# One ring of eight PSUM banks, the last batch's mixing among the first product's matmuls, and u's differences made in the front

## The chip, the cores and the metric

The kernel runs on one core of a Trainium2 chip. The metric is the device time of one execution in microseconds (us); the profiled span of an execution is 1.8 to 2.1 us shorter than its time.

## The reference, cut to what matters

Causal linear attention with decay (4 batches, 8 heads, 768 positions, head size 64), then a mixer: a low-rank product over the positions, and two large products with a ReLU between them.

```python
x = attention(q, k, v, lam)            # (4, 768, 512), heads side by side
h = x.transpose(0, 2, 1) @ U @ V       # rank 32, mixes the positions of one batch
u = x + h.transpose(0, 2, 1)
out = u + np.maximum(u @ w_ch1, 0.0) @ w_ch2     # 512 -> 2048 -> 512
```

## The kernel before

The kernel has a front (attention and mixing, in 24 steps of 128 positions), a first product (u with w_ch1) and a second. Both products are kept accurate by splitting an operand into a high part and a rest: two matmuls per block into pz, and a third into pd with the small difference u_d. Batches 0 and 1 run interleaved with a lag of one batch, and so do 2 and 3, so that one batch's attention lies beside the other's mixing.

The mixing of a batch and the turn of one step into the first product's operand:

```python
def tmp(name):                       # shared by pt, pt_h, ut, uf, wt, wl and others
    return wconv.tile([P, C], FP32, tag="tmp", bufs=3, name=name)
...
pts[b] = tmp("pt")                   # low(b): x times U for a batch, evicted by ScalarE
nc.scalar.copy(pts[b], pp)
...
nc.tensor.matmul(out=pr, lhsT=gather..., rhs=pts.pop(b), ...)      # low_sum(b)
t = tmp("pt_h")
nc.vector.tensor_scalar(t..., pr..., HI, None, ALU.bitwise_and)
nc.scalar.copy(p_hl[0 : P // 2], t[0 : P // 2])
nc.vector.tensor_tensor(out=p_hl[P // 2 : P], in0=pr[P // 2 : P], in1=t[P // 2 : P], op=ALU.subtract)
...
nc.tensor.matmul(out=pu, lhsT=v_hl[:, ...], rhs=p_hl, ...)         # mix(s)
nc.vector.tensor_tensor(out=xs[s], in0=pu, in1=xs[s], op=ALU.add)
...
pt = mbank([P, CT, P], "put")        # turn(s): four transposes of x_nat
t = tmp("ut")...
nc.vector.tensor_scalar(t..., pt..., HI, None, ALU.bitwise_and)
nc.scalar.copy(uhl[g][:, 0, :, cols], t)
nc.vector.tensor_tensor(out=uhl[g][:, 1, :, cols], in0=pt, in1=t, op=ALU.subtract)
```

PSUM in the front is three rings: two banks for scores, three for attention, three for the rest. The differences are made by VectorE when the first product begins, ahead of each pair's first unit:

```python
def u_diff(g):
    for ct in range(CT):
        nc.vector.scalar_tensor_tensor(ud[g][:, ct, :], hi[:, ct, :], E, low[:, ct, :],
                                       ALU.mult, ALU.subtract)
```

## Time and profile before

| | before |
|---|---|
| median of 4 runs (lowest to highest) | 737.38 us (735.95 to 738.01) |
| profiled span, granted clock | 736.8 us, 0.981 |
| first pu (batch 0's mixing begins) | 78.64 us |
| last transposes of u (put) of batch 1's mixing | 119.46 us |
| pr of the last batch (its mixing alone is left) | 174.23 us |
| first matmul pz of the first product | 187.71 us |

All boundaries are starts of instructions on TensorE's timeline. The time from the first pu to the last put of batch 1, 40.8 us here, is called the stretch below: two batches are mixed in it, beside the attention of one or two others.

### The profile page before, as it was taken

To read this page: it belongs to the slowest core of one execution; us is meant where nothing else is said; L and a number is where in the kernel's file an instruction comes from. 1 tells how busy PE (TensorE), PEld (TensorE's weight loads), DVE (VectorE), ACT (ScalarE), POOL (GpSimd) and SP (SyncE) were. 2 spreads that over 40 slices of the span, in tenths; PEclk is the share of its full clock that TensorE was granted. 3 is DMA by queue.
4 is the path that set the end of the run, shared out by engine and by line. 5 is a ranking of instruction groups with operands and counts; after the bars stand their busy time and mean duration, and the time that the engine had idled before them with its cause. 6 is when DMAs were issued, how large, how long until landed. Compare 5 with 4: busy or idle time off the path is not lost.

```text
span 736.8 us, 11337 instructions
## 1 busy us (share of the span) xinstructions
PE 706.1 (96%) x4176; PEld 567.9 (77%) x4176; DVE 514.3 (70%) x903; ACT 300.2 (41%) x525; POOL 87.6 (12%) x74
## 2 busy tenths in 40 slices
PE   5789999997899999999999999999999999999997
PEld 4677778874688888888888888888888888888885
DVE  4544997467999867777777924578668686676864
ACT  2554656655346555455445612223232232322320
POOL 2323214330300000000000000003002030110300
PEclk9979999998899999999999999999999999999999
DMA  9876767722247665556556689985536344363431
GB/s 155 172 158 156 188 163 183 156 76 103 97 143 269 232 213 186 210 190 223 194 211 228 229 314 309 346 314 167 162 90 211 96 159 146 101 187 100 159 98 57
DMA packets 131807, 131.76 MB, mean 179 GB/s; under 512 B 81320, under 2 KB 89512, under 8 KB 131752
## 3 DMA queue, kind: packets, MB, share of 16 engines
q1 hardware_dynamic: 131752, 131.04, 57.4%
q8 instruction: 33, 0.54, 0.3%
q14 instruction: 22, 0.18, 0.1%
HBM read 80.68 MB, written 50.33 MB: 178 GB/s over the span
## 4 chain that ended last, share of the span: by engine, by line
PE 87%; DVE 5%; ACT 3%; DMA 2%; issue 1%; POOL 1%; SPq 1%; DVEq 0%; ACTq 0%; POOLq 0%
PE pz L541 24%; PE pd L547 12%; PE pz L643 12%; PE pz L642 12%; PE pd L644 12%; PE ps L293 3%; PE px L315 3%; PE px L310 2%; DMA words<-in_moe_V_dram 1%; PE pk L261 1%; PE pkv L331 1%; DVE sm L298 1%; PE pq L261 1%; PE pxn L355 1%; PE put L405 1%
## 5 line engine op out<-in xcount | busy, mean ns | idle before, releaser
L541 PE MATMUL pz<-u_hl,w 128*128 128x512 f32 x768 | 187.8, 397 | 0.0
L541 PEld LDWEIGHTS pz<-u_hl,w 128*128 128x128 f32 x768 | 144.7, 189 | 35.2
L643 PE MATMUL pz<-w_hl,m 128*128 128x512 f32 x384 | 152.2, 396 | 0.0
L644 PE MATMUL pd<-w_d,m 128*128 128x512 f32 x384 | 152.2, 396 | 0.0
L642 PE MATMUL pz<-w_hl,m 128*128 128x512 f32 x384 | 152.2, 396 | 0.0
L627 ACT ACTIVATE m<-mt 128x512 fp32r<-128x512 f32 x96 | 60.6, 632 | 192.5 <-PE pd L644 132.3
L628 DVE SCALAR_TENSOR_TENSOR m<-rm,m 128x512 fp32r<-128x512 f32 x96 | 71.4, 746 | 50.6 <-ACT m L627 50.3
L555 DVE SCALAR_TENSOR_TENSOR r<-pd,r 128x512 f32<-128x512 f32 x96 | 61.7, 685 | 62.4 <-ACT r L554 54.1
L547 PE MATMUL pd<-u_d,w 128*128 128x512 f32 x384 | 99.4, 401 | 2.9 <-DVE u_d L530 2.9
L554 ACT ACTIVATE r<-pz 128x512 f32<-128x512 f32 x96 | 52.2, 596 | 109.0 <-PE pz L541 109.0
L547 PEld LDWEIGHTS pd<-u_d,w 128*128 128x128 f32 x384 | 73.2, 191 | 21.2 <-issue 3.4
L642 PEld LDWEIGHTS pz<-w_hl,m 128*128 128x128 f32 x384 | 72.3, 188 | 17.6
L644 PEld LDWEIGHTS pd<-w_d,m 128*128 128x128 f32 x384 | 72.3, 188 | 17.6
L643 PEld LDWEIGHTS pz<-w_hl,m 128*128 128x128 f32 x384 | 72.3, 188 | 17.6
L664 POOL TENSOR_TENSOR o<-o,u 128x512 f32<-128x512 f32 x20 | 29.8, 1523 | 468.6 <-DVE o L662 468.6
L629 DVE SCALAR_TENSOR_TENSOR m<-m 128x512 fp32r<-128x512 f32 x96 | 69.1, 721 | 0.9
L626 DVE TENSOR_SCALAR mt<-rm 128x512 uint32<-128x512 uint32 x96 | 46.1, 480 | 27.1 <-DMA rm<-r_d 26.6
L315 PE MATMUL px<-sm,vraw 128*64 128x128 f32 x384 | 38.6, 287 | 1.6 <-DVE sm L298 1.6
L298 DVE TENSOR_TENSOR sm<-ps,mask 128x1024 f32<-128x1024 f32 x24 | 29.3, 1220 | 13.7 <-PE ps L293 13.7
L271 POOL TENSOR_TENSOR qs<-qt,powq 128x512 f32<-128x512 f32 x20 | 26.0, 1302 | 96.5 <-PE px L310 58.5
L293 PE MATMUL ps<-qt,kt 64*128 64x128 f32 x384 | 32.4, 305 | 3.4 <-DVE sm L298 2.4
L310 PE MATMUL px<-qs,kv 128*64 128x128 f32 x320 | 34.4, 286 | 0.2 <-ACT kv L346 0.2
(79 smaller groups left out, 752.6 us busy)
## 6 DMA issues: line engine op xcount, KB each, us to landing
r_d<-r SPq DMA_DIRECT2D x96, 256.0 KB, 2.1
rm<-r_d SPq DMA_DIRECT2D x96, 256.0 KB, 2.6
words<-in_moe_w_ch_dram SPq DMA_DIRECT2D x32, 512.0 KB, 4.0
w_d<-w SPq DMA_DIRECT2D x16, 768.0 KB, 3.3
w_hl<-w_d SPq DMA_DIRECT2D x16, 512.0 KB, 5.8
qraw<-in_q_dram SPq DMA_DIRECT2D x24, 256.0 KB, 4.8
kraw<-in_k_dram SPq DMA_DIRECT2D x24, 256.0 KB, 4.0
vraw<-in_v_dram SPq DMA_DIRECT2D x24, 256.0 KB, 3.5
```

The source lines that it names most:

```text
L293: nc.tensor.matmul(out=ps[:, x, a, :], lhsT=kt[rows, a, :], rhs=qt[rows, a, :], start=True, stop=True,)
L315: nc.tensor.matmul(out=px[x * D : (x + 1) * D, a, :], lhsT=vr[:, 2 * a + x, :], rhs=sm[:, x, a, :], start=(c == 0), stop=True,)
L541: nc.tensor.matmul(out=acc[g][0], lhsT=w[:, n, ct, :], rhs=uhl[g][:, n, ct, :], start=(ct == 0 and n == 0), stop=(ct == CT - 1 and n == 1),)
L547: nc.tensor.matmul(out=acc[g][1], lhsT=w[:, 2, ct, :], rhs=ud[g][:, ct, :], start=(ct == 0), stop=(ct == CT - 1),)
L554: nc.scalar.mul(r, pz, 1.0 + E)
L555: nc.vector.scalar_tensor_tensor(r, pd, 4096.0, r, ALU.mult, ALU.add)
L627: nc.scalar.activation(out=m[:, 0], in_=t, func=AF.Relu)
L628: nc.vector.scalar_tensor_tensor(m[:, 1], r, 0.0, hi, ALU.max, ALU.subtract)
L629: nc.vector.scalar_tensor_tensor(m[:, 2], hi, E, low, ALU.mult, ALU.subtract)
L642: nc.tensor.matmul(out=pz, lhsT=m[:, 0, cols], rhs=hl[:, 0], start=first, stop=False)
L643: nc.tensor.matmul(out=pz, lhsT=m[:, 1, cols], rhs=hl[:, 1], start=False, stop=end)
L644: nc.tensor.matmul(out=pd, lhsT=m[:, 2, cols], rhs=dd, start=first, stop=end)
```

## The change

The intent: the last batch's mixing, which left TensorE idle and cool between the front and the first product, is placed among the first product's first four units. For the first product not to wait for VectorE, the differences of batches 0 to 2 are made in the turns of the front, from data that VectorE has just touched, and kept in DRAM until the first product loads them. PSUM becomes one ring of eight banks for the whole kernel, and the start is reordered. The diff, cut to its core:

```diff
-    ps_s = ... bufs=1 (two banks); ps_a = ... bufs=3; ps_m = ... bufs=3
+    ps = ctx.enter_context(tc.tile_pool(name="ps", bufs=8, space=bass.MemoryType.PSUM))
...
-        ps = ps_s.tile([P, 2, HP, P], FP32, tag="pss", name="ps")
+        pss = [bank([P, HP, P], "pss") for x in range(2)]
-        nc.vector.tensor_tensor(out=sm, in0=ps, in1=mask, op=ALU.mult)
+        for x in range(2):
+            nc.vector.tensor_tensor(out=sm[:, x], in0=pss[x], in1=mask[:, x], op=ALU.mult)
...  (turn)
+            diff = tmp("ud").rearrange("p (c n) -> p c n", n=P)
+        nc.vector.scalar_tensor_tensor(diff, t, 1.0 + E, pt, ALU.mult, ALU.subtract)
+        if not late:
+            nc.sync.dma_start(out=ud_d[g][:, :, cols], in_=diff)
...
+    merged = [piece for piece in merged if piece not in mixing(B - 1)]
...
+    for pair in ((0, 1), (2, 3), (4,)):
+        for ct in range(CT):
+            for g in pair:
+                nc.sync.dma_start(out=ud[g][:, ct, cols].bitcast(FP32), in_=ud_d[g][:, ct, cols])
-    def u_diff(g): ...
...  (start of the first product)
+    rest = mixing(B - 1)
+    at = [(0, 6), (0, 14), (0, 19), (1, 0), (1, 5), ...]      # (unit, matmul) of each piece
+        hidden(ft, pair, before)
```

## The prediction

> **What bounds the kernel now.** I read the page first (busy shares, then the 40 slices), then the table of windows by stage, then TensorE's and VectorE's timelines around the hand-over from the front (attention and mixing) to the first product.
>
> ```profile
> PE 706.1 (96%) x4176; PEld 567.9 (77%) x4176; DVE 514.3 (70%) x903; ACT 300.2 (41%) x525; POOL 87.6 (12%) x74
> PEclk9979999998899999999999999999999999999999
> L547 PE MATMUL pd<-u_d,w 128*128 128x512 f32 x384 | 99.4, 401 | 2.9 <-DVE u_d L530 2.9
> ```
>
> TensorE is busy 96% of the span, so the kernel is bound by it, and only time in which it idles or runs at the lower clock can be won. The clock row shows three dips, all in the first quarter. The third line shows the only wait inside the first product: 2.9 us for the differences u_d.
>
> The chain of work in order of time has one unit of the first product (16 + 8 matmuls of 512 columns) every 5.62 us, so 234 ns a matmul. 1152 of them are 269.8 us. The first starts at 187.71 (timeline), the second product's first at 462.2 (instructions that write pz), and the span ends at 736.8: the first product takes 274.5 us, 4.7 over its pure time, and everything from 462.2 on takes 274.6, of which 269.8 is again matmuls. There is nothing in the second half for this change. What remains is the front, 0 to 187.7, and the 4.7 us.
>
> ```profile
> 171.55 1.91 PE L367 MATMUL pp<-x_nat,u_w 128*32 128x512 f32 x12
> 173.40 0.66 PE L405 MATMUL put<-ident,x_nat 128*128 128x128 f32 x4
> 174.23 1.12 PE L376 MATMUL pr<-pt,gather 128*128 128x512 f32 x2 [0.18 <-ACT pt L372]
> 177.55 1.19 PE L390 MATMUL pu<-vp 128*128 128x512 f32 x2 [2.20 <-DVE vp L383]
> ...
> 186.15 1.80 PE L405 MATMUL put<-ident,x_nat 128*128 128x128 f32 x8 [0.42 <-ACT uf L414]
> 187.71 3.99 PE L541 MATMUL pz<-u_hl,w 128*128 128x512 f32 x16
> 191.53 0.39 PE L547 MATMUL pd<-u_d,w 128*128 128x512 f32 x1
> 194.87 3.24 PE L547 MATMUL pd<-u_d,w 128*128 128x512 f32 x7 [2.95 <-DVE u_d L530]
> ```
>
> From 174.2 to 187.7 TensorE has only the last batch's mixing: one product pr, six pu, six groups of four transposes. They are paced by a chain through VectorE, ScalarE and GpSimd, and TensorE falls to the low clock meanwhile (groups of four transposes take 1.05 to 1.12 us, against 0.60 when warm). Then eight pd matmuls wait for 16 u_d operations that VectorE has hardly begun.
>
> ```profile
> 80.00:100.00 20.00, 19.74 (x208) 14.52 (x204) 18.68 (x34) 12.23 (x23) 3.57 (x3) 1.00 0.78 211
> 100.00:120.00 20.00, 18.85 (x235) 15.99 (x234) 19.18 (x32) 12.60 (x24) 7.71 (x6) 1.00 0.64 171
> 130.00:140.00 10.00, 9.95 (x158) 9.10 (x156) 3.75 (x9) 6.61 (x14) 3.68 (x4) 1.00 1.00 204
> 160.00:170.00 10.00, 9.79 (x126) 8.07 (x123) 9.12 (x16) 5.82 (x12) 1.27 (x1) 1.00 0.22 80
> 400.00:450.00 50.00, 50.00 (x215) 40.20 (x214) 28.86 (x51) 19.94 (x36) 0.00 (x0) 1.00 0.79 284
> ```
>
> The columns are stretch, length, busy time of TensorE, its weight loads, VectorE, ScalarE, GpSimd, the granted clock, DMA share, GB/s. From 80 to 120, where two batches are mixed, VectorE is busy 37.9 of 40 us: it sets the pace there (matmuls "busy" include ones spaced out by waits: 443 in 40 us against 158 in 10 us later). At 130 to 140 TensorE sets it. At 160 to 170 both are near full.
>
> **What the Trainium skill says.** The page "TensorE: Matmul & The Clock Gate", section "What's actually happening", says that the array runs at half clock unless it was busy over a window of about 3.4 us. The trace agrees: the granted clock is 0.62 at 180 to 190 and 1.00 where TensorE is full. So a filled gap is worth more than its length. "VectorE: DVE Perf Modes", section on the TRN2 errata, gives (N+151)/0.96 ns for a float32 tensor_tensor, 691 ns at 512 elements; the u_d and u_hl operations here take 678 to 692. Back to back they overlap: 7 in 4.29 us, 0.61 each. "DMA: Bandwidth & Descriptors", "Why small descriptors are slow", gives a fixed cost per packet; here full engines would move 161/0.92 = 175 GB/s with the 256-byte packets of q, k and v at the start, but 284/0.79 = 360 GB/s at 400 to 450. That is 23 ns for 256 bytes and 91 for 2 KB on one of 16 engines; on a straight line, an estimate, 33 ns for 512 bytes. "PSUM — Partial Sum Buffer", "PSUM: the matmul accumulator", has 8 banks; both kernels use all 8.
>
> **The change, part by part.** Times are from where TensorE stands at 174.0 in the old trace (the third batch's last transposes and the fourth's pp done), because in the new order of TensorE's instructions the first pz follows exactly that point.
>
> (1) The mixing's idle time. Between 174.2 and 187.7 pass 13.5 us. The same work, warm, costs pr 0.94, six pu at 0.234 = 1.4, six transpose groups at 0.48 = 2.9, in sum 5.2 us, and it is still done, among matmuls. Gain 13.5 - 5.2 = 8.3.
>
> (2) The differences. 16 + 8 u_d operations after the hand-over go; the 4.7 us of waiting in the first product goes with them. Gain 4.7 at most.
>
> (3) New waits in the overlap. In the new order pu follows pr after four matmuls (0.94 us), while VectorE still has pt_h, one weight operation and vp to do (3 x 0.6 to 0.7, then a cast on ScalarE): about 1.7 us idle. The eight loads of the first pair's u_d (256 KB each) stand in the in-order DMA queue behind stores of the last differences and partly wait for attention buffers. At 0.73 us each on full engines (128 x 91 ns / 16) plus 2 us to land, they come about 7 us after the first pz; the matmuls want them from 5 to 7.5 us after. I allow 1 us there and 0.8 for transposes that wait for x_nat. Loss 3.5.
>
> (4) VectorE in the front. 18 of the 24 differences move there, 0.61 us each. Twelve fall in 75 to 122, where VectorE is the bound: 12 x 0.61 = 7.3, of which about 2 us of its idle time there may absorb one: loss 6. Six fall in 155 to 174, where VectorE has more than 10% free: 6 x 0.61 = 3.7, loss 2. The split of sm into two of 512 columns costs 2 x 0.61 against 1.13 between starts, 0.1 a step, which is inside these.
>
> (5) Their stores. A difference goes out in 512 packets of 512 bytes: 512 x 33 ns / 16 = 1.06 us of all engines. Twelve are 12.7 us in a stretch of 47 us with DMA at 0.71: just under full. Each keeps one of only three temporary buffers until it has landed (2.4 us and more), and the next-but-one turn needs that buffer. Where turns come 1.5 to 2.4 us apart, as around 118 to 121, VectorE waits. Loss 2, the least certain term.
>
> (6) The start. The first q is issued ahead of lam, the first scores no longer stand behind the second k in TensorE's order (it waited for that k at 9.84; scores began at 10.86), three sets of q, k and v are loaded ahead, and scores have separate banks. In the old trace 15 us go in idle time and low clock between 29 and 58 (a gap of 3.7 for q, one of 2.4 for sm, and some 14 us at about half speed after them), but DMA is at 0.92 and 0.83 until 40, so part is bandwidth that no order brings back. V's words now come two loads later, and VectorE waits for them ahead of a sm. Gain 5.
>
> Sum on the path: -8.3 - 4.7 + 3.5 + 6 + 2 + 2 - 5 = -4.5; from a median of 737.9 that is 733. Terms 4 to 6 could be one, as TensorE at 130 to 150 is bound by itself either way. I shade the sum by 3 us toward the gain, since losses (4) and (5) are taken as if they added up and partly they are the same wait: 730.
>
> **Rivals.** A: the hand-over is all, and the front keeps its length (the added VectorE work hides beside TensorE and DMA waits). For it: VectorE is busy only 119 of the first 188 us by the windows. Against it: 37.9 of 40 just where most is added. It would give 737.9 - 8.3 - 4.7 + 3.5 - 5 = 723. B: the front grows as much as the hand-over wins: stores of differences hold the three temporary buffers and saturate DMA, q and k come late, TensorE cools. For it: DMA at 0.64 to 0.83 there before anything is added. Against: loads run ahead by three, and DMA at 1.00 at 130 to 140 cost TensorE nothing. It would give 738 to 741. C: the overlap fails: the first pd's wait for loads in a queue blocked by stores, and the stall of 3 us moves to the start. For it: one in-order queue issues all; against: 16 matmuls and half the mixing stand ahead. It would give 734 to 736. D: the ring of eight banks in order of allocation makes TensorE wait where score and transpose banks were separate rings; a step with mixing takes about nine banks, so reuse is after 0.9 step, against 0.75 for the old three-bank ring of pq, pk, px and pkv. I expect no visible cost.
>
> **Range and chances.** Run to run the old kernel is within 2 us. The uncertain terms are (4) to (6), each with some 4 us either way: 721 to 738 should hold it 8 times in 10. Two per cent faster is 723.1 or less, which needs rival A or a start better by 10: 0.15. Slower by 2% (752.7) needs the front to grow by 25 us: 0.02. Within 2%: 0.83.
>
> **What would show it.** (1) Between the last low-rank product pp and the last transposes no gap over 2 us on TensorE, and the last batch's pu among pz. (2) No wait of pd on VectorE; from the first pz to the second product's start 276 to 280 us. (3) The first pz at 176 to 183. (4) VectorE over 90% busy through all of both mixings, and that stretch 5 to 9 us longer. (5) VectorE's ut operations waiting on DMA stores. (6) The third batch's first steps earlier relative to the start, and fewer low-clock slices before 60. I am wrong if the first pz comes before 174 (front not bound by VectorE) or after 186, or if the second product loses time.

## More of the kernel before

Below, "third part" means the differences in the front with their DRAM copies.

## The result, and the profile after

| | before | after |
|---|---|---|
| median of 4 runs | 737.38 us | 740.43 us (739.99 to 740.85) |
| ratio, 95% interval | | 1.0044 [1.0027, 1.0061] |
| profiled span, clock | 736.8, 0.981 | 738.6, 0.987 |
| first pu | 78.64 | 72.50 |
| stretch, first pu to last put of batch 1 | 40.8 | 55.0 |
| end of the front (old: 174.0, where the last batch's mixing alone is left; new: first pz) | 174.0 | 184.9 |
| from there to the end of the span | 562.8 | 553.7 |

Ratios are the mean time of one kernel's runs over that of the other's of the same rounds, so not quite the ratio of the medians. The time is within 2%, but 740.4 lies above the predicted range of 721 to 738.

The page of after, the three lines that answer to those of before in the prediction:

```profile
PE 701.1 (95%) x4176; PEld 563.4 (76%) x4176; DVE 519.0 (70%) x927; ACT 299.6 (41%) x525; POOL 87.1 (12%) x74
PEclk9989999999999999999999999999999999999999
L565 PE MATMUL pd<-u_d,w 128*128 128x512 f32 x384 | 99.0, 397 | 1.6 <-DMA u_d<-ud_d 1.6
```

The clock's dip at the hand-over (the two eights in the row of before) is gone, and 2.9 us of waiting for VectorE became 1.6 us of waiting for loads. TensorE is busy 5 us less, which fits the higher mean clock (0.987 against 0.981) but was not taken apart. All of this is the gain that was wanted. TensorE's timeline at the hand-over (start, length, operation, idle time before it and what ended that):

```profile
184.88 3.05 PE L558 MATMUL pz<-u_hl,w 128*128 128x512 f32 x12
187.76 1.02 PE L380 MATMUL pr<-pt,gather 128*128 128x512 f32 x2
188.22 1.50 PE L558 MATMUL pz<-u_hl,w 128*128 128x512 f32 x4
191.58 0.47 PE L394 MATMUL pu<-vp 128*128 128x512 f32 x1 [1.86 <-DVE vp L387]
...
193.97 0.51 PE L565 MATMUL pd<-u_d,w 128*128 128x512 f32 x1 [0.52 <-DMA u_d<-ud_d]
...
196.95 0.50 PE L565 MATMUL pd<-u_d,w 128*128 128x512 f32 x1 [1.10 <-DMA u_d<-ud_d]
```

The last batch's pr and pu lie among pz and pd, and the waits that are left are 3.5 us in sum, just what the prediction allowed. So the hand-over won 562.8 - 553.7 = 9.1 us. But the first pz came at 184.9 and not at 176 to 183: the front grew by 10.9 us. The windows by stage say where (columns as in the prediction):

```profile
80.00:100.00 20.00, 14.32 (x130) 8.85 (x127) 16.83 (x31) 7.65 (x14) 1.28 (x1) 0.91 0.66 188
100.00:120.00 20.00, 17.51 (x184) 14.46 (x184) 16.69 (x26) 9.40 (x17) 6.13 (x5) 0.91 0.71 184
```

TensorE does 314 matmuls there against 443 before. Yet VectorE, which was to be the bound, is less busy than before (33.5 against 37.9 us of 40), DMA is not full, and the clock is 0.91 where it was 1.00. Over 20 us nobody is at a limit. Windows of 4 us, some of which are shown under e2, tell more: VectorE is full where TensorE waits (busy 4.00 us at 96 to 100, TensorE 1.17) and has slack just after (2.58 at 104 to 108). The engines wait for each other in turn. TensorE's four long waits of the stretch in after:

```profile
87.46 0.40 PE L311 MATMUL px<-qs,kv 128*64 128x128 f32 x2 [2.85 <-ACT kv L347]
99.88 1.12 PE L380 MATMUL pr<-pt,gather 128*128 128x512 f32 x2 [2.83 <-ACT pt L376]
104.06 0.47 PE L394 MATMUL pu<-vp 128*128 128x512 f32 x1 [2.18 <-DVE vp L387]
121.91 0.66 PE L261 MATMUL pq<-ident,qraw 128*128 128x128 f32 x4 [2.22 <-DVE ud L426]
```

The second is for pt, ScalarE's copy of the small product, and pt itself waited. ScalarE's timeline:

```profile
97.79 0.62 ACT L414 CAST u_hl<-ut 128x512 fp32r<-128x512 f32 x1 [2.10 <-DVE ut L413]
99.24 0.58 ACT L376 COPY pt<-pp 128x512 f32<-128x512 f32 x1 [0.83 <-DMA ud_d<-ud]
```

The trace puts the end of pt's wait down to a store of a difference: pt's buffer is one of the three temporary ones, and a difference was in it. That reading, "the store holds the buffer", is the prediction's own term (5), and the first theory. The experiments had to tell it from the rivals: VectorE's extra operations, the ring of banks, and the new start.

### The profile page after: what moved, and what is told of

Its sections match the earlier page's. It is cut to its first block, busy times and chain, and to the rows that moved or that the text cites. A ratio compares the mean times of both kernels' runs of the same rounds, so it can differ in the third digit from the quotient of the medians.

```text
span 738.6 us, 11431 instructions
## 1 busy us (share of the span) xinstructions
PE 701.1 (95%) x4176; PEld 563.4 (76%) x4176; DVE 519.0 (70%) x927; ACT 299.6 (41%) x525; POOL 87.1 (12%) x74
## 4 chain that ended last, share of the span: by engine, by line
PE 86%; DMA 6%; DVE 5%; ACT 1%; issue 1%; SPq 0%; POOL 0%; DVEq 0%; ACTq 0%; POOLq 0%
PE pz L558 24%; PE pz L674 12%; PE pz L673 12%; PE pd L675 12%; PE pd L565 12%; PE px L316 2%; PE pss L293 2%; PE px L311 2%; PE pp L370 1%; PE put L409 1%; DMA words<-in_moe_V_dram 1%; DMA kraw<-in_k_dram 1%; PE pkv L332 1%; PE pq L261 1%; PE pk L261 1%; DMA ud_d<-ud 1%
## 5 line engine op out<-in xcount | busy, mean ns | idle before, releaser
L558 PE MATMUL pz<-u_hl,w 128*128 128x512 f32 x768 | 190.0, 398 | 0.0
L673 PEld LDWEIGHTS pz<-w_hl,m 128*128 128x128 f32 x384 | 72.3, 188 | 17.6
L675 PEld LDWEIGHTS pd<-w_d,m 128*128 128x128 f32 x384 | 72.3, 188 | 17.6
L674 PEld LDWEIGHTS pz<-w_hl,m 128*128 128x128 f32 x384 | 72.3, 188 | 17.6
L316 PE MATMUL px<-sm,vraw 128*64 128x128 f32 x384 | 40.3, 292 | 8.0 <-DMA vraw<-in_v_dram 6.8
L316 PEld LDWEIGHTS px<-sm,vraw 128*64 128x64 f32 x384 | 27.5, 148 | 11.4 <-DMA vraw<-in_v_dram 7.3
L299 DVE TENSOR_TENSOR sm<-pss,mask 128x512 f32<-128x512 f32 x48 | 30.5, 682 | 3.0 <-PE pss L293 2.8
```

What stands on the lines that cost most here:

```text
L316: nc.tensor.matmul(out=px[x * D : (x + 1) * D, a, :], lhsT=vr[:, 2 * a + x, :], rhs=sm[:, x, a, :], start=(c == 0), stop=True,)
L558: nc.tensor.matmul(out=acc[g][0], lhsT=w[:, n, ct, :], rhs=uhl[g][:, n, ct, :], start=(ct == 0 and n == 0), stop=(ct == CT - 1 and n == 1),)
L673: nc.tensor.matmul(out=pz, lhsT=m[:, 0, cols], rhs=hl[:, 0], start=first, stop=False)
L674: nc.tensor.matmul(out=pz, lhsT=m[:, 1, cols], rhs=hl[:, 1], start=False, stop=end)
L675: nc.tensor.matmul(out=pd, lhsT=m[:, 2, cols], rhs=dd, start=first, stop=end)
```

## The experiments

Seventeen runs were made, all correct: fifteen further kernels, and e1 and after once more. They fell in five sittings, each on one chip with its own runs of before (medians of before 735.9 to 738.2). The table has the boundaries of each profiled run and the timing. "End of front" is the first pz, or in the kernels with the old hand-over (marked o) the last batch's pr. "Rest" is the span less that. The changed kernel and the first experiment were each profiled twice; their stretches and their rests repeated within 0.1 us, but their first pu only within 2.2 and their ends of front within 1.9. So a difference of about 2 us in the first pu or the end of the front, between single profiles, settles nothing.

| run | first pu | stretch | end of front | rest | median | ratio to before |
|---|---|---|---|---|---|---|
| before (o) | 78.6 | 40.8 | 174.2 | 562.6 | 737.4 | |
| after | 72.5 | 55.0 | 184.9 | 553.7 | 740.4 | 1.0044 [1.0027, 1.0061] |
| e1 | 72.3 | 43.9 | 172.2 | 555.9 | 731.7 | 0.9918 [0.9887, 0.9949] |
| e2 | 73.5 | 49.1 | 179.4 | 551.5 | 734.4 | 0.9956 [0.9902, 1.0009] |
| e3 (o) | 76.7 | 45.3 | 177.2 | 564.6 | 743.3 | 1.0085 [1.0050, 1.0120] |
| e4 (o) | 79.2 | 45.2 | 181.2 | 562.2 | 743.8 | 1.0086 [1.0052, 1.0119] |
| e5 | 74.1 | 43.8 | 178.9 | 552.2 | 734.3 | 0.9968 [0.9935, 1.0000] |
| e6 | 75.6 | 50.6 | 187.9 | 551.4 | 740.3 | 1.0045 [1.0004, 1.0086] |
| e7 (o) | 73.6 | 43.1 | 172.6 | 560.8 | 735.1 | 0.9988 [0.9946, 1.0029] |
| e8 (o) | 77.1 | 40.8 | 172.5 | 562.5 | 736.6 | 1.0003 [0.9957, 1.0048] |
| e9 | 75.7 | 45.3 | 180.6 | 551.2 | 728.7 | 0.9903 [0.9867, 0.9938] |
| e10 | 76.0 | 43.9 | 179.3 | 553.5 | 733.2 | 0.9944 [0.9914, 0.9974] |
| e11 (e1 again) | 74.4 | 43.8 | 174.1 | 556.0 | 732.6 | 0.9947 [0.9914, 0.9981] |
| e12 (after again) | 74.6 | 54.9 | 185.8 | 553.6 | 741.4 | 1.0069 [1.0038, 1.0100] |
| e13 | 75.9 | 54.0 | 185.7 | 556.5 | 743.5 | 1.0086 [1.0058, 1.0114] |
| e14 | 74.1 | 55.1 | 185.7 | 556.9 | 744.4 | 1.0117 [1.0075, 1.0159] |
| e15 (o) | 71.2 | 46.5 | 174.8 | 563.0 | 739.5 | 1.0053 [1.0012, 1.0095] |
| e16 | 76.3 | 43.9 | 178.8 | 551.3 | 730.3 | 0.9913 [0.9888, 0.9938] |
| e17 | 73.8 | 52.7 | 182.2 | 552.2 | 737.2 | 1.0024 [0.9988, 1.0060] |

### e1: the third part undone

After, but with the differences made by VectorE in the product as before, and no copy in DRAM.

```diff
-            diff = tmp("ud").rearrange("p (c n) -> p c n", n=P)
-        nc.vector.scalar_tensor_tensor(diff, t, 1.0 + E, pt, ALU.mult, ALU.subtract)
-        if not late:
-            nc.sync.dma_start(out=ud_d[g][:, :, cols], in_=diff)
...
+            if ft == 0:
+                for g in pair:
+                    u_diff(g)
```

> The changed kernel with its third part undone: no difference is made in the front and none goes to DRAM; VectorE makes u_d from u_hl ahead of each pair's first unit, as before. The overlap of the mixing, the ring of eight banks and the new order of the start stay. Theory V (VectorE's twelve added differences lengthen the stretch in which two batches are mixed, from 41 to 55 us): that stretch falls back to 41 to 44 us, the first pz comes at 172 to 176, pd waits 3 to 6 us for u_d, and the time is 729 to 733. Theory B (stores of differences hold the three temporary buffers): the same, it needs the next runs to be told from V. Theory R (the ring of banks and the new order of instructions lengthen the stretch, not the differences): the stretch stays at 52 to 55 us and the time at 739 to 745.

The stretch fell from 55.0 to 43.9 us and the time to 731.7. The third part thus costs the stretch 11.1 us, and the change without it is faster than both kernels by about 1%. What it loses is at the hand-over, where the last batch's pu now stands behind the differences in VectorE's order:

```profile
182.65 0.77 PE L393 MATMUL pu<-vp 128*128 128x512 f32 x1 [3.67 <-DVE vp L386]
```

(from its second profiling). This is what the third part was to avoid, and its worth: the rest is 555.9 us here and 553.7 in after.

### e2: the differences through staging buffers of their own

After, with the differences written to eight buffers of their own in memory that is free in the front, and not to the three shared ones.

```diff
+    stage = hl_pool.tile([P, 8, C], FP32, tag="hl", name="stage")
-            diff = tmp("ud").rearrange("p (c n) -> p c n", n=P)
+            diff = stage[:, s % 8].rearrange("p (c n) -> p c n", n=P)
```

> The changed kernel, with the differences of the front written to eight buffers of their own (in a u_hl buffer that is unused until the last batch) in place of the three temporary buffers; same operations, same stores. Theory B: the waits on the stores go, the stretch of the two mixings falls by 4 us or more, time 733 to 736. Theory V: VectorE's work is the same, the stretch falls by less than 2.5 us, time 738 to 740. Theory R: as V.

The stretch is 49.1 us: 5.9 less than after, with the same operations and the same stores. The other 5.2 of the 11.1 are the operations and their stores (e2 against e1). So sharing the three buffers costs a little more than all of VectorE's new work. The stretch as one window, for e1, e2 and after, shows that the two halves differ in kind (VectorE's busy time is the third after the length):

```profile
72.25:116.15 43.90, 40.74 (x467) 31.86 (x467) 39.72 (x72) 24.94 (x47) 11.94 (x10) 1.00 0.67 178
73.50:122.61 49.11, 42.07 (x467) 32.24 (x467) 44.92 (x81) 25.53 (x48) 11.25 (x10) 0.97 0.74 198
72.50:127.53 55.03, 44.94 (x467) 34.91 (x467) 47.10 (x82) 25.77 (x48) 10.09 (x9) 0.91 0.67 182
```

From e1 to e2 VectorE is busy 5.2 us longer and idle 4.2 us in both: the stretch grows by just what VectorE is given to do. From e2 to after its busy time grows by 2.2 us and its idle time from 4.2 to 7.9: that is waiting. Windows of 4 us show how far the difference reaches. First after, then e2:

```profile
100.00:104.00 4.00, 1.88 (x10) 1.11 (x10) 3.40 (x6) 1.99 (x4) 0.00 (x0) 1.00 0.28 80
104.00:108.00 4.00, 3.94 (x28) 3.43 (x29) 2.58 (x4) 0.90 (x2) 0.15 (x1) 0.71 1.00 248
108.00:112.00 4.00, 4.00 (x54) 3.23 (x53) 2.91 (x5) 2.38 (x5) 2.17 (x2) 0.86 0.55 154
...
124.00:128.00 4.00, 4.00 (x53) 3.87 (x52) 3.31 (x8) 1.43 (x4) 0.70 (x1) 0.73 0.76 197
```

```profile
104.00:108.00 4.00, 4.00 (x58) 3.57 (x54) 3.93 (x7) 1.54 (x3) 1.29 (x2) 1.00 0.80 200
108.00:112.00 4.00, 4.00 (x40) 3.39 (x42) 4.00 (x8) 2.79 (x7) 1.05 (x1) 1.00 0.77 198
```

The column to read is the granted clock, third from the end. In after it falls to 0.71 and 0.86 behind the two waits at 97 to 104, and again behind the wait at 122; in e2 it stays at 1.00, and 58 matmuls go through where after has 28. Over the windows from 100 to 128 the clock's deficit in after sums to 4 x (0.29 + 0.14 + 0.15 + 0.27) = 3.4 us (the 0.15 is the window 120 to 124, not shown). (The window 88 to 92 is low in both, 0.58 and 0.57, behind the wait for kv, which is 2.85 us in after and 2.78 in e2; in e1 that wait is 1.05 and the clock 1.00.) TensorE's other three long waits, in e2, which sum to 4.1 us against 7.2 in after:

```profile
98.52 1.13 PE L381 MATMUL pr<-pt,gather 128*128 128x512 f32 x2 [0.68 <-ACT pt L377]
103.01 0.47 PE L395 MATMUL pu<-vp 128*128 128x512 f32 x1 [2.49 <-DVE vp L388]
118.08 0.66 PE L262 MATMUL pq<-ident,qraw 128*128 128x128 f32 x4 [0.93 <-DVE stage L427]
```

3.1 us of longer waits and 3.4 us of low clock, 6.5 together, are roughly the 5.9. That the clock falls because of the waits is an inference from their order in time. Sharing costs at the hand-over too: the rest is 551.5 us in e2 and 553.7 and 553.6 in the two profiles of after, where pu waits 1.9 us and pd 1.6 and 1.4; in e2 pu does not wait there and pd waits 0.6.

### e3 and e4: the operations, and operations with stores, in the old order

Before, with the eighteen differences in the turns, into the shared buffers and never read (e3), and with their stores to DRAM too (e4).

```diff
+            diff = tmp("ud").rearrange("p (c n) -> p c n", n=P)
+            nc.vector.scalar_tensor_tensor(diff, t, 1.0 + E, pt, ALU.mult, ALU.subtract)
+            nc.sync.dma_start(out=ud_d[g][:, :, cols], in_=diff)        # e4 only
```

> The kernel before, with one added VectorE operation in each of the first 18 turns: the same difference, from PSUM, into a temporary buffer, read by nothing; the old u_d stays. Theory V: twelve of them at 0.61 us fall where VectorE is the bound, the front grows by 6 to 9 us, time 744 to 747. Theory B: no store, so under 3 us, 738 to 741. Theory R: as B.

> The run before this one, with the store of each added difference to DRAM as well (512-byte packets, the temporary buffer held until it lands). Theory V: within 2 us of the run without the stores, 744 to 748. Theory B: 5 us or more above it. The gap between the two runs is the cost of the stores and of the buffers they hold.

The operations lengthen the stretch by 4.5 us and the time by 0.85%; the stores add nothing (45.2 against 45.3 us, 743.8 against 743.3), although they go through the same three buffers. The time of e3 fits no theory's range: it lies just below V's 744 to 747 and above the 738 to 741 of the others. The gap between e3 and e4 spoke against the first theory, or for something in the new order that makes the stores hurt.

### e5 and e6: two ways to take the operations off VectorE's full stretch

e5 is e2 with the first two batches' twelve differences moved behind both mixings, where VectorE is idle more than half of the time (the quiet stretch). A piece, in the edit below, is one call in the kernel's interleaved order, such as a turn. e6 is e2 with the low half of u in every turn made by ScalarE and GpSimd, as the last batch's is, so that VectorE does as many operations in a turn as before.

```diff
 e5
+    at = merged.index(("turn", QUIET - 1)) + 2
+    for j in range(QUIET):
+        merged.insert(at + 3 * j, ("diff", j))
 e6
+        uf = tmp("uf").rearrange("p (c n) -> p c n", n=P)
+        nc.scalar.copy(uf, pt)
+        nc.gpsimd.tensor_tensor(out=uhl[g][:, 1, :, cols], in0=uf, in1=t, op=ALU.subtract)
-            nc.vector.tensor_tensor(out=uhl[g][:, 1, :, cols], in0=pt, in1=t, op=ALU.subtract)
```

> The changed kernel with the staging buffers of the second run, and the differences of the first two batches moved in time: not in their turns, but as twelve operations from u_hl in SBUF in the stretch after both mixings, where VectorE is under 40% busy. Same number of VectorE operations, same bytes to DRAM. If V and B together explain the loss, the stretch of the two mixings falls to 41 to 45 us (55 in the changed kernel, 44 without differences, 49 with staging), the first pz comes at 172 to 175 and pd finds its data: 726 to 729, below the run with u_diff back (731.7). If theory R (ring, order of instructions) holds the rest, the stretch stays 3 us over that of before.

> The staging run, with the low half of u made by ScalarE's copy and GpSimd's subtraction in every turn (as only the last batch's turns do), so that VectorE has as many operations in a front turn as before the change. Theory V: the stretch falls from 49 to 43 to 46 us, time 728 to 731. If VectorE's count is not what matters, or GpSimd's operations hold up VectorE's, it stays at 49 or grows, time 734 or more.

e5 missed; of e6 the second case came, not the hoped-for one. In e5 the stretch fell to 43.8 us as expected, but twelve differences in eight staging buffers made VectorE itself wait for the stores, with the score masks behind it in its order:

```profile
141.31 1.37 DVE L437 SCALAR_TENSOR_TENSOR stage<-u_hl 128x512 f32<-128x512 f32 x1 [5.29 <-DMA ud_d<-stage]
```

The first pz came at 178.9 and nearly all was given back (734.3 us). In e6 the stretch was 50.6, no shorter than e2's, and the time 740.3: now VectorE waits for the other two engines, for example

```profile
102.04 0.69 DVE L414 TENSOR_SCALAR ut<-put 128x512 uint32<-128x512 uint32 x1 [0.56 <-POOL u_hl L419]
103.90 0.69 DVE L425 SCALAR_TENSOR_TENSOR stage<-ut,put 128x512 f32<-128x512 f32 x1 [0.57 <-ACT uf L418]
```

and the first of these is a wait for a shared temporary buffer again, which uf, a fourth kind of tile in the turn, now rotates through.

### e7 and e8: the ring of banks alone, the new start alone

Before with only the front's PSUM as one ring of eight banks and sm in two halves (e7); before with only the new order of loads and constants at the start (e8).

```diff
 e7
-    ps_s = ... ; ps_a = ... ; ps_m = ...
+    ps_f = front_ctx.enter_context(tc.tile_pool(name="ps_f", bufs=8, space=bass.MemoryType.PSUM))
 e8
+    load_next("q")
+    nc.sync.dma_start(out=lamb, in_=lam.unsqueeze(0).broadcast_to([P, H]))
+    load_next("k")
+    load_next("v")
```

> The kernel before with one ring of eight PSUM banks in the front in place of three pools, which splits sm in two operations of 512 columns; nothing else. Theory R: the stretch of the two mixings, 40.8 us before, grows by 3 us or more and so does the time. My prediction took it for free: within 1.5 us of before.

> The kernel before with the new order of the start alone: q ahead of lam, three sets of q, k and v loaded ahead, constants in two parts. The prediction gave 5 us to the whole of the new start; if the loads' order earns them, the first pu comes 4 to 6 us earlier than 78.6 and the time falls by as much, 732 to 734. If it is the ring's separate score banks or bandwidth, under 2 us.

The earlier first pu comes mostly from the ring: 5.0 us earlier in e7, 1.5 in e8, which is within what two profiles of one kernel differ by. But neither shortens the kernel (0.9988 and 1.0003): e7's stretch is 2.3 us longer, and at the last batch's pr only 1.6 us of its 5.0 are left. The stretch starts earlier and waits longer.

### e9, e10, e11, e12: a version that keeps the intent, beside e1 and after

e9 makes only the first pair's eight differences in the quiet stretch, each in a staging buffer of its own, so that no store is ever waited for; the other sixteen are made by VectorE in the product. e10 does the same for the first pair, makes group 2's four in the product, and keeps the differences of steps 12 on in their turns, as after has them. e11 and e12 are e1 and after once more, for a comparison on one chip.

```diff
 e9
+    at = merged.index(("turn", 2 * NT - 1)) + 4
+    for j in range(2 * CT):
+        merged.insert(at + 3 * j, ("diff", j))
...
+        if i == 1:
+            for g in pair:
+                u_diff(g)
 e10
+        if s >= QUIET:
+            nc.vector.scalar_tensor_tensor(diff, t, 1.0 + E, pt, ALU.mult, ALU.subtract)
```

> After, with no difference in any step of the front: the eight differences of the first pair are made in the quiet stretch between the mixings (each to its own staging buffer, stored, and loaded for the first product), the other sixteen made by VectorE in the first product from u_hl. If the cost of the change lay in the difference operations inside the two-batch mixing and in their stores holding temporary buffers, the stretch from first pu to last put is 43 to 45 us as in the first experiment (43.9), the first pz starts at 172 to 175, and the wait of pu for VectorE's vp at the hand-over (3.7 us there) is gone or under 2: 726 to 729. If VectorE's order blocks again (the score masks behind differences that wait for buffers, or the late turns behind the second pair's differences), 731 to 735.

> As the run above, but the differences of the third batch's six steps from 12 to 17 and of the last batch are made in their turns as in after, with staging buffers for the stores that stay. Same theory: stretch 43 to 45 us; the six in-turn differences cost at most 2 us before the first pz (174 to 177): 727 to 731. If it is 733 or more, differences in the late turns cost too, or VectorE's order blocks again.

> The first experiment's kernel once more beside the others on one chip, as the measure for them: 730 to 733, faster than before by 0.6 to 1.0 per cent.

> The changed kernel itself on the same chip, for a direct comparison: 739 to 742, slower than before by 0.3 to 0.6 per cent.

e9 has the best median, 728.7 us, as its theory expected, and its rest is 551.2: the wait of pu at the hand-over is gone. But the first pz of its profiled run came at 180.6, not at 172 to 175, because the eight differences lengthen the quiet stretch (from the last put of batch 1 to the first pz pass 59.6 us, against 56.0 in both profiles of e1's kernel); that run was the slowest of six (733.9). Its interval overlaps that of e11 on the same chip, so e9 beats before and after, but that it beats e1 is not settled. e10 is at 733.2, the case for which its expectation says that differences in the late turns cost too, or that VectorE's order blocks again. Its profile shows no cost in the front beside e9's, whose first pz is no earlier (179.3 against 180.6). The rest is 2.3 us longer, and in it pd waits 1.8 us for its loads of u_d, where e9 has no such wait. Why the medians lie 4.5 us apart stays open, since both profiled runs are the slowest of their six. e11 and e12 repeat in sign: after is slower than before, the change without its third part is faster. Their sizes, 0.5 and 0.7%, lie just outside the expected 0.6 to 1.0 and 0.3 to 0.6.

### e13 and e14: the store taken apart from the buffer

e1 with the eighteen differences added in the turns, into the shared temporary buffers, never read (e13), and stored as well (e14). This is the test of the first theory in the new order.

```diff
+            diff = tmp("ud").rearrange("p (c n) -> p c n", n=P)
+            nc.vector.scalar_tensor_tensor(diff, t, 1.0 + E, pt, ALU.mult, ALU.subtract)
+            nc.sync.dma_start(out=ud_d[g][:, :, cols], in_=diff)        # e14 only
```

> The first experiment's kernel (u's differences back on VectorE in the product) with the 18 difference operations added to the front's turns, into one of the three temporary buffers each, stored nowhere and never read (right result). If it is the store in flight that holds a temporary buffer and lengthens after's stretch from the first pu to the last put (55.0 us, against 49.1 with staging buffers), the stretch here is 48 to 50 us. If the mere rotation of a fourth kind of tile through three buffers is enough, it is 53 to 56.

> The same with the store of each difference from its temporary buffer to DRAM, never loaded again. In-flight stores: 53 to 56 us in the stretch, and the time 4 to 7 us over the run above. If stores cost nothing, as in the old arrangement (45.2 against 45.3), 48 to 50 us and the same time.

The first theory fell. Without any store the stretch is 54.0 us, 10.1 over e1, and the time 743.5; the stores add 1.1 us in the stretch and nothing that the intervals separate. It is not a store in flight that costs, it is that the differences take turns in the three shared buffers at all. What the sharing changes can be read from the order on ScalarE, first in e2 (own buffers), then in e13 (shared, no store):

```profile
97.88 0.59 ACT L377 COPY pt<-pp 128x512 f32<-128x512 f32 x1 [1.39 <-PE pp L371]
98.36 1.14 ACT L415 CAST u_hl<-ut 128x512 fp32r<-128x512 f32 x2
```

```profile
100.43 0.62 ACT L413 CAST u_hl<-ut 128x512 fp32r<-128x512 f32 x1 [1.50 <-DVE ut L412]
100.96 0.58 ACT L375 COPY pt<-pp 128x512 f32<-128x512 f32 x1
```

In e2, pt follows its product at once and the two copies of u come after. In e13 the build has put pt behind one of these copies, which waits 1.5 us for VectorE, and that one stands behind a difference. From the end of the product pp to the first pu of the batch pass 5.2 us in e2, 6.4 in e13 and 7.0 in after. The clock falls in e13 as in after (0.58 at 108 to 112).

### e15: is it the ring that makes the sharing hurt?

e7 with the operations and stores of e4.

> Before with the ring of eight banks alone (stretch 43.1) and the 18 difference operations with their stores through the temporary buffers. If it is the ring that lets the stores hurt (a step runs further ahead, so that the buffer is wanted while its store is in flight), the stretch is 52 us or more and the time 745 or more. If it needs the rest of the new order too (three loads ahead, the new start), it is 47 to 49 as sum of the parts (43.1 + 4.5) and the time 739 to 743.

Not by itself: the stretch is 46.5 us, 3.4 over e7, and the time 739.5. The clock is 1.00 in every window from 80 to 128 (0.73 at 72 to 76, behind a wait of 3.5 us that ends with the first pu), and no later wait of TensorE in the stretch is longer than 1.7 us. So in two kernels with the old hand-over the operations and stores in the shared buffers cost 4.4 us (e4) and 3.4 (e15), no more than the 5.2 that they cost with own buffers in the new order, where sharing adds 5.9. That sharing is harmless in the old order is inferred from this: no kernel with the old hand-over and own buffers was run. Which part of the new order is needed was not taken apart further, and a shared ring of more than three buffers was not tried.

### e16: the quiet differences further apart

e9 with one difference in every fifth piece instead of every third (`at + 5 * j`), begun two pieces later.

> As the kernel with the first pair's eight differences in the quiet stretch, but every fifth piece instead of every third. If the burst of eight on VectorE held up the score masks there (the quiet stretch grew from 33.2 to 36.9 us), half of that comes back: first pz 1 to 3 us earlier than 180.6 and 726 to 729 us. If VectorE's bursts are not the cause, no change: 728 to 731.

The first pz came 1.8 us earlier than in e9's profiled run, within what was expected, but the time did not follow: 730.3 us, ratio 0.9913 against 0.9903. The spacing is not what is left of the loss.

### e17: pt out of the shared buffers

After, with only pt and pt_h given buffers of their own; ut and the differences still share the three, and are stored.

```diff
+    own = hl_pool.tile([P, 8, C], FP32, tag="hl", name="own")
-            pts[b] = tmp("pt")
+            pts[b] = own[:, b % 2]
-        t = tmp("pt_h")
+        t = own[:, 2 + b % 2]
```

> The changed kernel with the two small-product tiles pt and pt_h in buffers of their own; ut and the differences rotate through the three temporary buffers and are stored as in after. If after's extra 5.9 us in the stretch come from pt having to wait for one of the three buffers, so that pr and pu come late, TensorE idles and its clock falls, then the wait ahead of the second batch's pr shrinks from 2.8 us to under 1, the clock stays at 1.00 between 100 and 112 us, the stretch is 48 to 52 us and the time 734 to 738. If it is the rotation of ut and the differences against each other, the stretch stays at 54 to 56 and the time at 739 to 742.

Half a hit. The wait ahead of pr shrank as expected, and the stretch by 2.3 us to 52.7; the time, 737.2, lies between after's and e2's, though its interval overlaps after's:

```profile
98.97 1.12 PE L382 MATMUL pr<-own,gather 128*128 128x512 f32 x2 [0.68 <-ACT own L378]
103.49 0.58 PE L396 MATMUL pu<-vp 128*128 128x512 f32 x1 [2.52 <-DVE vp L389]
121.94 0.65 PE L263 MATMUL pq<-ident,qraw 128*128 128x128 f32 x4 [2.90 <-ACT x_nat L360]
```

But the clock still fell to 0.61 for one window behind the wait of 2.52 us, which in e2 is 2.49 and cost no clock, and the third wait is 2.9 us against 0.9. So the places of pt and pt_h in the shared ring account for about 2.3 of the 5.9 us, and the remaining 3.6 belong to the other tiles that rotate there, ut against the differences among them; through which of their waits stays open.

## Why the prediction was wrong

**The hand-over, terms (1) to (3), was right.** They sum to -9.5 us, and the measured rest shrank by 9.1. No wait over 2 us, 3.5 us of new waits, and from the first pz to the second product 279.1 us were all as written. (The prediction's 174.0 is used for before here; by the start of pr, 174.2, the rest shrank by 8.9.) The match of the waits is not all merit: in e2, with own buffers, they are 0.6 us.

**The front, terms (4) to (6), was predicted at +5 (179.0 for the first pz) and measured at +10.9 (184.9).** The step whose mechanism failed is term (5), "their stores": 2 us, called the least certain. A second, term (6), failed on the path (below). Its buffer was the right one and its mechanism the wrong one. It had VectorE wait for a buffer until a store had landed; the stores cost 1.1 us (e14 against e13), and its own sign, ut waiting for stores, is not there: in the whole of after the waits put down to these stores are three, of pt 0.8 us, of ut 0.5 (after the stretch) and of a difference 0.5. What it left out is that pt, ut, pt_h and the weights' tiles share these buffers: one more tile in the rotation moves pt and the turns in the engines' orders, TensorE's waits grow by 3.1 us, and the clock gives back another 3.4. In all 5.9 us (after against e2). With own buffers the first pz is at 179.4, where the sum of the terms had it, and the time 734.4, near the unshaded sum of 733. That is partly luck: the front without differences ends at 172.2 and 174.1 in the two profiles of e1's kernel, so term (6) gave 2.0 or 0.1 us there and not 5, and the differences with own buffers cost 7.2 or 5.3 us and not the 10 of terms (4) and (5).

**Shading 733 to 730** was the second error. The reason given, that losses (4) and (5) were partly the same wait, did not hold in the new order: (4) measured 5.2 us with the buffers apart, and the buffers put 5.9 on top, more than the 2 of (5).

**Term (4) was right for its first half**: 6 us predicted for the stretch, 5.2 measured by e2 less e1, 4.5 by e3. Its mechanism holds too where the buffers are apart, as VectorE's idle time is the same in e1 and e2. Its second half was allowed 2. From the end of the stretch to the first pz after takes 57.4 us (56.3 in e12), 2.8 longer than before, but e1's kernel takes 56.0 without any difference, so the six differences cost 0.3 to 1.4 and the rest of the new order 1.5.

**Term (6) had the right size only at the start of the mixing, and failed on the path.** The first pu came 6.1 us earlier, for a predicted 5, but by the ring (e7) more than by the new start (e8). Of it 2.0 or 0.1 us were left at the end of the front (e1, e11), and in neither e7 nor e8 did it reach the median time. This miss of 3 to 5 us is as large as that of term (5).

**Rival D, the ring, had "no visible cost".** It adds 2.3 us to the stretch (e7) and the rest of the new order 0.8 (e1). That is no net loss, as the ring brings its own earlier start, but it means that the measured stretch, 14.2 us longer where 5 to 9 were predicted, is the sum of 40.8 + 2.3 + 0.8 + 5.2 + 5.9 = 55.0, where the prediction had 40.8 + 6 + 2. (These are differences of runs taken in this order, so they add up by construction.)

**Rival B** ("the front grows as much as the hand-over wins") names what came about, and its 738 to 741 holds the result. Its reasons were half wrong: DMA is at 0.66 to 0.71 in the stretch by windows of 20 us, not saturated, and no store needs to be in flight.

**The sign that failed**: point (4) of what would show it expected VectorE over 90% busy. It was 33.5 us of 40. Where the engine called the bound turns out less busy than before and the stage is longer, look for waits between engines. Adding up busy times predicted e2, where VectorE is busy 44.9 of 49.1 us, and could not predict after, where it is 47.1 of 55.0.

A small slip of reading, on which nothing rests: the third dip of the clock row is the eleventh slice, 184 to 203 us, just beyond the first quarter.

## What to carry to other kernels

Before a new tile goes into a small shared ring of buffers, list every other tile in that ring and ask which of them lies on a chain between engines; a new kind of tile delays those, even if nothing ever waits for the new tile itself. The Trainium skill's page "Perfetto Trace Analysis", section "Optimization Strategy", says that a repeating gap on the engine that should be saturated can mean that there isn't enough memory for the next tile; here the gap showed two steps further on, at TensorE's pr, as a wait for ScalarE. And waits on TensorE can be paid twice, in the wait and in the low clock seen after it: "TensorE: Matmul & The Clock Gate", section "What's actually happening", says that the activity window runs freely and that the point of change depends on where in it work falls, which fits that nearly equal waits (2.49 and 2.52 us) cost no clock in e2 and a window at 0.61 in e17; no run tests it. So spend spare memory on own buffers first, and move work between engines afterwards.

## What the Trainium skill lacked or had wrong

- "Perfetto Trace Analysis": it names too few buffers as a cause of gaps, but not that tiles of different kinds in one ring reorder the engines' work. Putting the differences in the three shared buffers costs 4.9 us in a stretch of 49 even without any store (e13 against e2), and 1.1 more with the stores (e14).
- "TensorE: Matmul & The Clock Gate": it puts the cost of warming up at under 1% of a typical span. Here the granted clock over the whole span is 0.981 before and 0.987 after, so 1.9 and 1.3% of it is missing, in several dips and not one ramp. From 100 to 128 us alone after loses 3.4 us, more than the whole difference between the two kernels (3.05 us in the medians), so it cannot be left out where small changes are judged.
- "VectorE: DVE Perf Modes", section on the TRN2 errata: its formula for a float32 tensor_tensor gives 691 ns at 512 elements, and the differences, a scalar_tensor_tensor of the same size, took 669 to 689, so it is close. It is no measure of what an operation adds to a full stretch: ten of the differences lie in e2's stretch, and VectorE's busy time there is 5.2 us longer than in e1's, about 0.52 each, with its idle time unchanged.
- No page: an earlier start of a stage by 5.0 us (e7) left 1.6 us at the end of the front and nothing in the time.
